# Pooled attention and capacity-limited experts on one core: another order for attention's first tiles

## Chip, core and metric

The kernel runs on one core of a Trainium2 chip. The metric is the device time of one execution in microseconds (us): 589.03 us is the median of three runs of the kernel before, which lie between 588.83 and 589.18 us. Times "at" a number are us from the start of the profiled span.

## The reference

Eight batch entries of q, k and v, each with 8 heads, 576 positions and 64 dims, go through attention against keys and values that are averaged over 8 positions (576 become 72):

```python
k_p = k.reshape(B, H, Sp, pool, D).mean(axis=3)
v_p = v.reshape(B, H, Sp, pool, D).mean(axis=3)
scores = scale * np.matmul(q, k_p.transpose(0, 1, 3, 2))
attn = np.exp(scores - scores.max(-1)) ; attn /= attn.sum(-1)
attn_out = np.matmul(attn, v_p)
```

The result, 4608 tokens of 512 numbers, goes to a mixture of 8 experts. Logits `x @ w_gate` are sorted over all tokens and experts, each expert takes at most 576 tokens, each token goes to one expert, and each expert computes `relu(x @ w1[e]) @ w2[e]` for its tokens.

## The kernel before

**Attention** works on 36 tiles of 128 tokens, in order. A batch entry is 4.5 tiles, so every ninth tile boundary falls on an entry's end, and tiles 4, 13, 22 and 31 hold the end of one entry and the beginning of the next. For tile n the steps are, with the names that the profile uses:

- `st_s` (scores): 4 matmuls of q (`rawq`) against the pooled keys in block-diagonal form (`kblk`), into the PSUM tile `pss`, of which there is one. The next tile's scores can only start when this tile's have been read.
- `softmax`: VectorE (DVE in the profile) takes the maximum (`mx`) and subtracts it (`e`), ScalarE (ACT) takes the exponential.
- `st_e`: five transposes of `e` through TensorE (PE), three into `pse`, two into `rt`, and a copy of each group to SBUF (`eT`) by ScalarE.
- `st_av`: five matmuls of `eT` against the masked pooled values (`vblk`, with the gate's 8 columns and a column for the sum of the weights) into one of two tiles `psa`.
- `norm`: VectorE divides by the sum (`rinv`, `gt`, every fourth tile `lg`, and `xt`); ScalarE's queue stores the tile.

In the loop over n, PE's queue holds `st_s(n)`, `st_e(n-1)`, `st_av(n-2)`, and VectorE's `mx(n)`, `e(n)`, `norm(n-3)`. Everything is written by hand in this order (a manual schedule), and each engine executes its own queue in order. A wait at the head of a queue holds up all that stands behind it.

**Pooling.** k, v and q of an entry are loaded by SyncE's queue (SP). The keys of an entry (`rawk`, 128 x 4 x 8 x 72) are summed in three steps, lines 173, 174 and 177; the last writes `kblk`. The values (`rawv`, 128 x 5 x 512, five chunks) are summed in three steps, lines 186 to 188 (`t`, `t`, `vsum`); three masked products, line 196, spread `vsum` over `vblk`. `prep_v` (three transposes of `vsum`, L209, and ScalarE's copy `vT`) and `prep_g` (three matmuls with the gate's weights, L218, and VectorE's product L219, "put" below) make the gate's columns of `vblk`. GpSimd (POOL) does k and v of entries 1 to 7. For entry 0, VectorE pools three quarters of k, TensorE the fourth (`add_k`); VectorE pools chunks 0 to 2 of v, and TensorE, with an identity matrix, chunks 3 and 4 (`add_v`, L156, with ScalarE's `put_v`).

**Constants** for the routing that follows are made in `consts` (before k of entry 0 is pooled) and `more` (after it), mostly on VectorE.

**After attention** come routing (a search for each expert's threshold) and the experts' matmuls, lines 1178 to 1266. Neither is touched.

Of the kernel before, what the change touches and what calls it, by code (L numbers as in the profile page):

```python
# [22 lines left out]
class Attention:  # L23
# [102 lines left out]
    def cut(self, b):  # L126

        return 256 + 64 * (b % 2)
# [7 lines left out]
    def q_of(self, b, j, n, m):  # L136

        c = self.cut(b)
        o = j * c + n if n < c else 4 * c + j * (self.S - c) + n - c
        return self.qT[b][:, o:o + m]  # L140
# [11 lines left out]
    def add_v(self, b, c):  # L152

        ps = self.ps0[:, 1, 128:256].rearrange("p (c d) -> p c d", c=2)
        for t in range(8):
            self.nc.tensor.matmul(ps, self.ident, self.rv[b][:, c, 64 * t:64 * t + 64], start=(t == 0), stop=(t == 7))  # L156

    def put_v(self, b, c):
        nc, B = self.nc, self.BLOCKS
        ps = self.ps0[:, 1, 128:256].rearrange("p (c d) -> p c d", c=2)  # L160
        self.sums[b] = self.wk.tile([128, 5, 64], F32, name="vsum")
        nc.scalar.activation(self.sums[b][:, c], ps, AF.Copy)
        for m in range(c.start, c.stop):
            for n in range(B[m], B[m + 1]):
                nc.scalar.activation(self.vblk[b % 4][:, n, :64], ps[:, m - c.start], AF.Copy, scale=self.mask[:, n:n + 1])

    def pool_k(self, b, eng, halves=(slice(0, 4),)):

        src = self.rk.pop(b)
        t1 = self.wk.tile([128, 4, 4, 72], F32, name="tk1", bufs=1)  # L170
        t2 = self.wk.tile([128, 4, 2, 72], F32, name="tk2", bufs=1)
# [7 lines left out]
    def pool_v(self, b, eng, c=slice(0, 5), blocks=None):  # L179
# [3 lines left out]
        t1 = self.wk.tile([128, 5, 256], F32, name="t1", bufs=1)  # L183
        t2 = self.wk.tile([128, 5, 128], F32, name="t2", bufs=1)
        s, v, B = self.sums[b], self.vblk[b % 4], self.BLOCKS
# [27 lines left out]
    def prep_g(self, b):  # L213
# [115 lines left out]
    def run(self, ctx, full, consts, more, after, end, warm):  # L329
# [7 lines left out]
        self.pS, self.e, self.eT, self.pA = {}, {}, {}, {}  # L337
        nt, B, S = self.nt, self.B, self.S
# [7 lines left out]
        mid = {}  # L346

        kh = (slice(0, 2), slice(2, 4))
        vh = (slice(0, 3), slice(3, 5))
        n = 4 * self.cut(0)  # L350
        self.load_k(0, kh)
        self.load_q(0, slice(0, n))
        self.load_v(0, vh[::-1])
# [1393 lines left out]
```

## Time and profile before

| | |
|---|---|
| median of three runs | 589.03 us |
| profiled execution | 588.63 us |
| its span, first to last instruction | 586.8 us |
| TensorE busy | 570.1 us (97% of the span) |
| VectorE, ScalarE, GpSimd busy | 392.1, 264.9, 176.5 us |
| mean granted TensorE clock | 0.987 |

The span leaves out 1.8 us of the execution. A busy share says how long an engine had an instruction in it, with overlaps; it doesn't say that the engine set the time in a given stage. For that the reader needs the order in time: which engine stood still, and what it stood still for. The rows further down are taken from the timeline (start, duration, engine, line, operation, output<-input, and in brackets the idle time before it and what ended it), from groups by line, from the chain of waits, and from the DMA issues.

### The profile page before, as it was taken

The numbers are of one execution on the slowest core, as the hardware profiler recorded it, in microseconds if no ns is written. First come the engines' busy times: TensorE is split into PE (matmuls) and PEld (weight loads), VectorE is DVE, ScalarE is ACT, GpSimd is POOL, SyncE is SP. The second block draws the span as 40 slices with busy tenths as digits, with TensorE's granted clock in tenths as the row PEclk, the third lists the DMA queues.
The fourth block names the chain that finished last, engine by engine and source line by source line (L and its number), as shares of the span: only waits on it lengthen the run. The fifth ranks groups of instructions, "written<-read, shape, count | busy, mean of one in ns | idle before, by whom it ended". The sixth has DMA issues, their size and how long they took to land.

```text
span 586.8 us, 10400 instructions
## 1 busy us (share of the span) xinstructions
PE 570.1 (97%) x3699; PEld 469.3 (80%) x3699; DVE 392.1 (67%) x1145; ACT 264.9 (45%) x528; POOL 176.5 (30%) x222
## 2 busy tenths in 40 slices
PE   8999999995999999999999999999999999999996
PEld 5999999893798889879976777678768868876874
DVE  7677878898897779687964886396658517421500
ACT  6444545444462445453462455246325724642401
POOL 1999999300300510420312302130121123011012
PEclk9999999997899999999999999999999999999999
DMA  8999982122550875568373926574484749165011
GB/s 352 421 422 422 396 349 80 77 83 72 169 196 3 267 192 174 165 180 286 110 167 89 360 67 161 181 269 123 94 298 132 165 152 327 57 162 196 12 41 45
DMA packets 74204, 110.25 MB, mean 188 GB/s; under 512 B 40640, under 2 KB 40640, under 8 KB 71456
## 3 DMA queue, kind: packets, MB, share of 16 engines
q1 hardware_dynamic: 62864, 81.02, 41.8%
q0 software_dynamic: 5952, 19.01, 9.6%
q10 hardware_dynamic: 5328, 9.48, 4.2%
q8 instruction: 30, 0.49, 0.3%
q14 instruction: 30, 0.25, 0.1%
HBM read 72.53 MB, written 27.92 MB: 171 GB/s over the span
## 4 chain that ended last, share of the span: by engine, by line
PE 79%; issue 6%; DVE 5%; POOL 4%; DMA 3%; ACT 0%; SPq 0%; POOLq 0%; another core or an unknown queue 0%; DVEq 0%; ACTq 0%
PE h L1261 25%; PE h L1215 16%; PE h L1178 14%; PE psa L273 6%; PE pss L228 5%; PE h L1266 4%; PE h L1204 3%; DMA rawk<-in_k_dram 2%; PE pse L257 1%; PE rt L666 1%; PE rt L257 1%; POOL tk L173 1%; DMA out_dram<-yt,rows 1%; DVE marks L659 1%; PE rt L218 1%
## 5 line engine op out<-in xcount | busy, mean ns | idle before, releaser
L1261 PE MATMUL h<-w2l,hh 128*128 128x512 f32 x256 | 101.0, 395 | 0.0
L1261 PE MATMUL h<-w2h,hh 128*128 128x512 f32 x256 | 100.7, 393 | 0.1
L1261 PE MATMUL h<-w2h,hl 128*128 128x512 f32 x256 | 100.8, 394 | 0.0
L1241 POOL DMA_INDIRECT out_dram<-yt,rows x29 | 28.9, 995 | 227.8 <-ACT yt L1275 227.3
L1090 POOL DMA_INDIRECT xg<-xd,rows x40 | 39.8, 996 | 85.8 <-ACT w1h L1098 28.1
L273 PE MATMUL psa<-vblk,eT 128*128 128x146 f32 (+3 forms) x390 | 60.0, 302 | 0.2
L1102 DVE TENSOR_TENSOR w1l<-raw,w1h 128x512 fp32r<-128x512 f32 x64 | 41.8, 685 | 24.4 <-ACT w1h L1098 23.9
L1261 PEld LDWEIGHTS h<-w2h,hh 128*128 128x128 f32 x256 | 48.2, 188 | 9.8 <-issue 0.5
L1261 PEld LDWEIGHTS h<-w2l,hh 128*128 128x128 f32 x256 | 48.2, 188 | 9.3
L1261 PEld LDWEIGHTS h<-w2h,hl 128*128 128x128 f32 x256 | 48.2, 188 | 9.2
L1275 ACT ACTIVATE yt<-h 128x512 f32<-128x512 f32 x32 | 19.0, 595 | 78.4 <-PE h L1261 54.7
L1220 ACT ACTIVATE hh<-h 128x512 fp32r<-128x512 f32 x40 | 23.9, 598 | 64.6 <-PE h L1215 64.6
L273 PEld LDWEIGHTS psa<-vblk,eT 128*128 128x128 f32 (+1 forms) x390 | 50.9, 180 | 1.8 <-POOL kblk L177 0.3
L1215 PE MATMUL h<-xh,w1h 128*128 128x512 f32 x160 | 45.2, 397 | 0.0
L1221 DVE SCALAR_TENSOR_TENSOR hl<-h,hh 128x512 fp32r<-128x512 f32 x40 | 27.4, 684 | 26.5 <-ACT hh L1220 26.4
L228 PE MATMUL pss<-kblk,rawq 128*128 128x144 f32 (+1 forms) x320 | 43.7, 294 | 1.4 <-DVE e L239 1.2
L1215 PE MATMUL h<-xl,w1h 128*128 128x512 f32 x160 | 43.8, 392 | 0.0
L1215 PE MATMUL h<-xh,w1l 128*128 128x512 f32 x160 | 43.6, 392 | 0.0
L1111 DVE TENSOR_TENSOR w2l<-raw,w2h 128x512 fp32r<-128x512 f32 x64 | 42.4, 681 | 0.0
L1098 ACT ACTIVATE w1h<-raw 128x512 fp32r<-128x512 f32 x64 | 37.0, 625 | 11.4 <-DMA raw<-in_moe_w_dram 11.2
L228 PEld LDWEIGHTS pss<-kblk,rawq 128*128 128x128 f32 (+1 forms) x320 | 37.0, 179 | 4.5 <-issue 2.5
L1108 ACT ACTIVATE w2h<-raw 128x512 fp32r<-128x512 f32 x64 | 37.9, 626 | 0.0
(240 smaller groups left out, 1107.0 us busy)
## 6 DMA issues: line engine op xcount, KB each, us to landing
raw<-in_moe_w_dram SPq DMA_DIRECT2D x64, 512.0 KB, 6.5
xd<-xt ACTq DMA_DIRECT2D x36, 256.0 KB, 3.9
rawv<-in_v_dram SPq DMA_DIRECT2D x7, 1280.0 KB, 13.7
rawk<-in_k_dram SPq DMA_DIRECT2D x7, 1152.0 KB, 12.9
rawq<-in_q_dram SPq DMA_DIRECT2D x7, 1152.0 KB, 10.2
xs<-planes SPq DMA_DIRECT2D x31, 256.0 KB, 2.9
rawk<-in_k_dram SPq DMA_DIRECT2D x2, 576.0 KB, 4.8
xs<-planes SPq DMA_DIRECT2D x7, 128.0 KB, 2.7
```

The source lines that it names most:

```text
L228: nc.tensor.matmul(ps[cols, j // 2, 144 * (j % 2):144 * (j % 2) + 144], self.q_of(b, j, n, cols.stop - cols.start), self.kblk[b % 4][:, j] ...
L273: self.nc.tensor.matmul(o[h], self.eT[i][:, c, h], self.vblk[b % 4][:, self.BLOCKS[c]:self.BLOCKS[c + 1]], start=(c == cs[0]), stop=(c == ...
L1090: nc.gpsimd.indirect_dma_start(out=self.xg[:n, t, :], out_offset=None, in_=self.xd, in_offset=bass.IndirectOffsetOnAxis(ap=rows[:n, t:t + ...
L1098: self.nc.scalar.activation(h, raw, AF.Copy)
L1102: self.nc.vector.tensor_tensor(l, raw, h.bitcast(F32), op=OP.subtract)
L1108: self.nc.scalar.activation(self.w2h[:, i], self.raw2[e][:, i], AF.Copy)
L1111: self.nc.vector.tensor_tensor(self.w2l[:, i], self.raw2[e][:, i], self.w2h[:, i].bitcast(F32), op=OP.subtract)
L1178: nc.tensor.matmul(ps[:, :m], a[:, n % 4, fs], b[:, n % 4, o], start=(n == 0), stop=(n == 11))
L1215: nc.tensor.matmul(ps, a[:, j, fs], b[:, j, :512], start=(n == 0), stop=(n == 11))
L1221: later(0.85, 0.69, lambda f=f, ps=ps: nc.vector.scalar_tensor_tensor(hl[:, f, :512], ps, 0.0, hh[:, f, :512].bitcast(F32), op0=OP.max, op ...
L1241: st = nc.gpsimd.indirect_dma_start(out=rows, out_offset=bass.IndirectOffsetOnAxis(ap=idx, axis=0), in_=y, in_offset=None)
L1261: nc.tensor.matmul(ps, a[:, f, o], b[:, f], start=(f == 0 and k == 0), stop=(f == 7 and k == 2))
```

## The change

q of entry 0 comes in three pieces instead of two (tokens 0 to 255, 256 to 383, the rest); the second now stands in front of v. For entry 1 q's first piece stands in front of v. Scores of tiles 0, 1 and 2 are issued in a row, tile 1's into a tile `psa`. `add_v` and `put_v` are gone: GpSimd pools chunks 3 and 4 and then 1 and 2 of entry 0's v, VectorE chunk 0. Of entry 1, VectorE pools the second half of k and chunk 4 of v, GpSimd the rest. `st_av` of tiles 0 and 1 follow after the scores of tile 3. `most` is the maximum alone, so that a put can stand between maximum and subtraction. Entry 2's `prep_v` and `prep_g` move one tile later. Constants of `consts` and `more` go to GpSimd, apart from three integer operations that VectorE now does before it pools k.

```diff
+    def cuts(b, S):
+        return (0, 256, 384, S) if not b else (0, 256 + 64 * (b % 2), S)
...
+    def most(self, i):
         ps = self.pS.pop(i)[:, :, :288].rearrange("p g (h y) -> p g h y", h=4)
         mx = self.wk.tile([128, 2, 4], F32, name="mx")
+        self.nc.vector.tensor_reduce(mx, ps, axis=AX.X, op=OP.max)
+        self.mx[i] = ps, mx
...
-        self.load_q(0, slice(0, n))
+        self.load_q(0, slice(0, 1024), slice(1024, 1536))
         self.load_v(0, vh[::-1])
-        self.load_q(0, slice(n, 4 * S))
+        self.load_q(0, slice(1536, 4 * S))
...
+        self.load_k(1)
+        self.load_q(1, slice(0, n))
+        self.load_v(1)
+        self.load_q(1, slice(n, 4 * S))
...
+            plan(n, self.pool_k, b, nc.gpsimd, (slice(0, 4 if b > 1 else 2),))
+            plan(n, self.pool_v, b, nc.gpsimd, slice(0, 5 if b > 1 else 4))
...
+        self.st_s(0)
+        self.st_s(1, "psa", 2)
+        self.pool_v(0, nc.gpsimd, vh[1])
+        self.pool_v(0, nc.gpsimd, slice(1, 3))
+        self.softmax(0)
+        self.st_s(2)
+        self.softmax(1)
+        self.pool_v(0, nc.vector, slice(0, 1))
+        self.blocks(0)
+        for n in range(2):
...
+            self.st_e(n, 0)
+            self.st_e(n, 1)
+        self.prep_v(0)
+        self.softmax(2)
+        self.st_s(3)
+        put = self.prep_g(0)
+        self.most(3)
+        put()
+        self.st_e(2, 0)
+        self.st_e(2, 1)
+        self.st_av(0, 0)
+        self.st_av(0, 1)
+        self.softmax(3)
+        self.pool_k(1, nc.vector, kh[1:])
+        self.st_av(1, 0)
+        self.st_av(1, 1)
+        self.norm(0)
+        self.pool_v(1, nc.vector, slice(4, 5))
+        self.blocks(1)
...
+        at_v = {first[b] + (b == 2): b for b in range(2, B)}
+        at_g = {first[b] + 1 + (b <= 2): b for b in range(1, B)}
+        for n in range(4, nt):
             self.st_s(n)
...
-        nc.vector.tensor_scalar(self.tri, jp, 0.0, None, op0=OP.is_gt)
+        nc.gpsimd.tensor_scalar(self.tri, jp, 0.0, None, op0=OP.is_gt)
```

First place: VectorE's queue from the last constants (before) and from the last keys (after) up to the third tile. `td`, `dq`, `tq` and `qcol` are constants of the routing, `t_` and `vsum` belong to the pooling of v, `mx` and `e` to the softmax. Before:

```order
L521 TENSOR_SCALAR td<-jp 128x4
L523 TENSOR_SCALAR dq<-td 128x4
L525 TENSOR_SCALAR tq<-pq 128x1
L527 TENSOR_SCALAR qcol<-tq 128x1
L238 TENSOR_REDUCE mx<-pss 128x8
L239 TENSOR_TENSOR e<-pss,mx 128x576
L186 TENSOR_TENSOR t_308<-rawv 128x768
L187 TENSOR_TENSOR t_309<-t_308 128x384
L188 TENSOR_TENSOR vsum<-t_309 128x192
L238 TENSOR_REDUCE mx<-pss 128x8
L239 TENSOR_TENSOR e<-pss,mx 128x576
```

And in the changed kernel:

```order
L168 TENSOR_TENSOR kblk_137<-tk_241 64x72 x2
L229 TENSOR_REDUCE mx<-pss 128x8
L238 TENSOR_TENSOR e<-pss,mx 128x576
L229 TENSOR_REDUCE mx<-psa 128x8
L238 TENSOR_TENSOR e<-psa,mx 128x576
L177 TENSOR_TENSOR t_289<-rawv 128x256
L178 TENSOR_TENSOR t_290<-t_289 128x128
L179 TENSOR_TENSOR vsum<-t_290 128x64
L229 TENSOR_REDUCE mx<-pss 128x8
L238 TENSOR_TENSOR e<-pss,mx 128x576
L229 TENSOR_REDUCE mx<-pss 128x8
```

The constants no longer stand between the keys and the first maximum, the pooling of v is a third as wide, and it has moved behind the second softmax.

Second place: VectorE's queue around the first `norm` (RECIPROCAL, `gt`, `xt`) and the maximum of tile 4. Before:

```order
L285 RECIPROCAL rinv<-psa 128x8
L288 TENSOR_TENSOR gt_432<-psa,rinv 128x64
L298 TENSOR_TENSOR xt<-psa,rinv 128x512
L238 TENSOR_REDUCE mx<-pss 128x8
L239 TENSOR_TENSOR e<-pss,mx 128x576
```

And in the changed kernel (`tk_` and `kblk_138` are entry 1's keys):

```order
L164 TENSOR_TENSOR tk_327<-rawk 128x576
L165 TENSOR_TENSOR tk_328<-tk_327 128x288
L168 TENSOR_TENSOR kblk_138<-tk_328 64x2x72 x2
L284 RECIPROCAL rinv<-psa 128x8
L287 TENSOR_TENSOR gt_405<-psa,rinv 128x64
L297 TENSOR_TENSOR xt<-psa,rinv 128x512
L177 TENSOR_TENSOR t_334<-rawv 128x256
L178 TENSOR_TENSOR t_335<-t_334 128x128
L179 TENSOR_TENSOR vsum<-t_335 128x64
L229 TENSOR_REDUCE mx<-pss 128x8
L238 TENSOR_TENSOR e<-pss,mx 128x576
```

Four instructions on entry 1's keys and three on its values now stand in front of tile 4's maximum.

Third place: SyncE's queue, the loads of entries 0 and 1. Before:

```order
L134 DMA rawq<-in_q_dram 128x1024
L124 DMA rawv<-in_v_dram 128x1024
L124 DMA rawv<-in_v_dram 128x1536
L134 DMA rawq<-in_q_dram 128x1280
L119 DMA rawk<-in_k_dram 128x2304
L124 DMA rawv<-in_v_dram 128x2560
L134 DMA rawq<-in_q_dram 128x2304
```

And in the changed kernel:

```order
L135 DMA rawq<-in_q_dram 128x1024
L135 DMA rawq<-in_q_dram 128x512
L124 DMA rawv<-in_v_dram 128x1024
L124 DMA rawv<-in_v_dram 128x1536
L135 DMA rawq<-in_q_dram 128x768
L119 DMA rawk<-in_k_dram 128x2304
L135 DMA rawq<-in_q_dram 128x1280
L124 DMA rawv<-in_v_dram 128x2560
L135 DMA rawq<-in_q_dram 128x1024
```

A piece of 128 x 512 (0.26 MB) stands before entry 0's v, and one of 128 x 1280 (0.66 MB) before entry 1's.

## Rows read from the trace of the kernel before

**Rows 1.** The page: busy time by engine; TensorE's granted clock in 40 equal slices of the span, in tenths; and the chain that ended last, by engine.

```profile
PE 570.1 (97%) x3699; PEld 469.3 (80%) x3699; DVE 392.1 (67%) x1145; ACT 264.9 (45%) x528; POOL 176.5 (30%) x222
...
PEclk9999999997899999999999999999999999999999
...
PE 79%; issue 6%; DVE 5%; POOL 4%; DMA 3%; ACT 0%; SPq 0%; POOLq 0%; another core or an unknown queue 0%; DVEq 0%; ACTq 0%
```

**Rows 2.** The chain of waits in order of time, its first long pieces: start, duration, what.

```profile
3.83 11.98 DMA rawk<-in_k_dram
15.88 2.63 POOL tk L173
...
21.80 2.91 POOL t L186
```

**Rows 3.** The timeline of the first 30 us: the first scores, VectorE from the last constants on, and the second scores.

```profile
7.95 1.29 PE L228 MATMUL pss<-kblk,rawq 128*128 128x144 f32 x8
...
8.26 0.23 DVE L492 TENSOR_SCALAR tri<-jp 128x128 bf16<-128x128 int32 x1
...
10.48 0.15 DVE L527 TENSOR_SCALAR qcol<-tq 128x1 f32<-128x1 int32 x1
...
10.56 0.75 DVE L238 TENSOR_REDUCE mx<-pss 128x8 f32<-128x576 f32 x1
11.34 0.76 DVE L239 TENSOR_TENSOR e<-pss,mx 128x576 f32<-128x576 f32 x1
12.01 0.95 DVE L186 TENSOR_TENSOR t<-rawv 128x768 f32<-128x768 f32 x1
...
12.24 1.22 PE L228 MATMUL pss<-kblk,rawq 128*128 128x144 f32 x8 [1.21 <-DVE e L239]
```

**Rows 4.** The timeline of TensorE's matmuls from 14 to 36 us (L228 scores, L257 transposes, L273 values, L209 and L218 the gate's columns), and the scores of tile 13.

```profile
21.92 1.20 PE L228 MATMUL pss<-kblk,rawq 128*64 128x144 f32 x16
23.05 0.60 PE L257 MATMUL pse<-ident,e 128*127 128x128 f32 x3
23.48 1.04 PE L273 MATMUL psa<-vblk,eT 128*128 128x146 f32 x6
24.36 0.38 PE L257 MATMUL rt<-ident,e 128*127 128x128 f32 x2
24.57 0.67 PE L273 MATMUL psa<-vblk,eT 128*128 128x146 f32 x4
25.08 1.14 PE L228 MATMUL pss<-kblk,rawq 128*128 128x144 f32 x8
...
28.27 0.52 PE L209 MATMUL rt<-ident,vsum 128*128 128x128 f32 x3
28.62 1.15 PE L228 MATMUL pss<-kblk,rawq 128*128 128x144 f32 x8
29.61 0.49 PE L257 MATMUL pse<-ident,e 128*127 128x128 f32 x3
29.94 0.74 PE L218 MATMUL rt<-wblk,vT 128*128 128x40 f32 x6
30.61 1.56 PE L273 MATMUL psa<-vblk,eT 128*64 128x146 f32 x12
...
33.17 1.25 PE L228 MATMUL pss<-kblk,rawq 128*128 128x144 f32 x8
...
52.68 1.24 PE L228 MATMUL pss<-kblk,rawq 128*64 128x144 f32 x16
```

**Rows 5.** GpSimd's pooling: the first line of k with the shortest, median and longest of its seven instructions in ns, two lines of v (busy us, mean ns), and the three masked products of entry 1 in the timeline.

```profile
L173 POOL TENSOR_TENSOR tk<-rawk x7: 2622/2628/2644, 15.9 to 94.4; 128x1152 f32<-128x1152 f32 x7
...
L186 POOL TENSOR_TENSOR t<-rawv 128x1280 f32<-128x1280 f32 x7 | 20.3, 2907 | 0.6
...
L187 POOL TENSOR_TENSOR t<-t 128x640 f32<-128x640 f32 x7 | 10.8, 1541 | 0.5
...
27.35 1.66 POOL L196 TENSOR_TENSOR vblk<-vsum,mask 128x128 f32<-128x128 f32 x3
```

**Rows 6.** SyncE's issues in order of time (start, duration): the two pieces of entry 0's v, and entry 3's v, which takes over the completion semaphore of entry 1's q and so is issued when that q has landed. Then two loads with us from issue to landing: the first piece of entry 0's v (issued at 2.17) and entry 2's k (issued at 6.08).

```profile
2.17 1.13 SPq L124 DMA_DIRECT2D rawv<-in_v_dram  x2
...
21.83 0.33 SPq L124 DMA_DIRECT2D rawv<-in_v_dram  x1
...
rawv<-in_v_dram SPq DMA_DIRECT2D x1, 512.0 KB, 6.5
...
rawk<-in_k_dram SPq DMA_DIRECT2D x1, 1152.0 KB, 18.8
```

**Rows 7.** The table by stretches: busy us by engine (instructions), granted clock, DMA's busy share and GB/s.

```profile
60.00:110.00 50.00, 49.94 (x408) 47.62 (x408) 41.03 (x90) 23.42 (x49) 46.60 (x39) 1.00 0.62 243
```

**Rows 8.** VectorE: the subtraction and two steps of the keys by form (busy us, mean ns), and the first and the last instruction of a `norm` in the timeline.

```profile
L239 DVE TENSOR_TENSOR e<-pss,mx 128x576 f32<-128x576 f32 x30 | 22.7, 758 | 2.9
...
L173 DVE TENSOR_TENSOR tk<-rawk 128x576 f32<-128x576 f32 x1 | 0.8, 758 | 0.0
...
L174 DVE TENSOR_TENSOR tk<-tk 128x288 f32<-128x288 f32 x1 | 0.5, 457 | 0.0
...
21.57 0.20 DVE L285 RECIPROCAL rinv<-psa 128x8 f32<-128x8 f32 x1
...
21.94 0.68 DVE L298 TENSOR_TENSOR xt<-psa,rinv 128x512 f32<-128x512 f32 x1
```

More of the change, by code (lines that the diff above doesn't have):

```diff
@@ L136, in q_of @@
     def q_of(self, b, j, n, m):
-        c = self.cut(b)
-        o = j * c + n if n < c else 4 * c + j * (self.S - c) + n - c
+        cuts = self.cuts(b, self.S)
+        for c0, c1 in zip(cuts, cuts[1:]):
+            if n < c1:
+                break
+        o = 4 * c0 + j * (c1 - c0) + n - c0
         return self.qT[b][:, o:o + m]
@@ L150, in add_k @@
             nc.scalar.activation(self.kblk[b % 4][h, j, y], ps[h], AF.Copy)
[L152 to L165, printed above, removed]
-    def pool_k(self, b, eng, halves=(slice(0, 4),)):
-        src = self.rk.pop(b)
-        t1 = self.wk.tile([128, 4, 4, 72], F32, name="tk1", bufs=1)
-        t2 = self.wk.tile([128, 4, 2, 72], F32, name="tk2", bufs=1)
+    def pool_k(self, b, eng, halves=(slice(0, 4),)):
+        src = self.rk[b]
+        if b not in self.tk:
+            self.tk[b] = (self.wk.tile([128, 4, 4, 72], F32, name="tk1", bufs=1),
+                          self.wk.tile([128, 4, 2, 72], F32, name="tk2", bufs=1))
+        t1, t2 = self.tk[b]
         for c in halves:
@@ L380, in run @@
             plan(first[b - 3] + 1, self.load_q, b)
-        for n in range(nt):
-            if n == 2:
-                self.prep_g(0)
-            self.st_s(n)
-            if n == 0:
-                self.add_v(0, vh[1])
-            for f in mid.get(n, ()):
-                f()
-            both = n >= 2 and len(self.parts(n - 2)) > 1 and n != first[1] + 2
-            if n >= 1:
-                self.st_e(n - 1, 0)
-            if n == first[1] + 2:
-                self.prep_g(1)
-            if n >= 2 and not both:
+        self.st_s(0)
@@ new lines, in run @@
+        self.most(3)
[11 more added lines that the diff above has]
+        self.blocks(1)
+        for n in (2, 3):
+            for f, a in at.get(n, ()):
+                f(*a)
+        at_v = {first[b] + (b == 2): b for b in range(2, B)}
@@ L396, in run @@
+        at_g = {first[b] + 1 + (b <= 2): b for b in range(1, B)}
+        for n in range(4, nt):
+            self.st_s(n)
+            both = len(self.parts(n - 2)) > 1
+            if n in at_v:
+                self.prep_v(at_v[n])
+            if n in at_g:
+                put = self.prep_g(at_g[n])
+                if n - 2 in first:
+                    self.most(n)
+                put()
+            self.st_e(n - 1, 0)
+            if not both:
                 self.st_av(n - 2, 0)
-            if n >= 1:
-                self.st_e(n - 1, 1)
+            self.st_e(n - 1, 1)
@@ L399, in run @@
             if both:
                 self.st_av(n - 2, 0)
[L401 to L404 removed]
+            self.st_av(n - 2, 1)
+            if n == first[1] + 1:
+                self.prep_v(1)
             self.softmax(n)
[L406 to L412 removed]
+            self.norm(n - 3)
@@ L413, in run @@
+            for f in after.get(n - 3, ()):
+                f()
             for f, a in at.get(n, ()):
```

121 lines of the change are left out of this document (55 added, 66 removed).

## The prediction

> **What bounds the kernel now.** I read the page first: TensorE is busy for 97% of the span and leads the chain for 79% of it [rows 1]. That doesn't tell whether attention's first 30 us, where everything that changes lies, are bound by it. So next the chain in order of time: from 3.8 to 29 us it doesn't run through TensorE but through the load of entry 1's k, which lands at 15.8, and then through GpSimd, which pools that k and, from 21.80, entry 1's v [rows 2]. Last the timelines. At the start VectorE is late: the first scores end at 7.95+1.29 = 9.24, but the maximum over them starts at 10.56, behind constants that run from 8.26 to 10.63, and the second scores wait until 12.24 for the subtraction [rows 3]. From 21.92 on TensorE runs without a gap worth the name, one tile in 3.1 us (21.92 to 25.08), up to 28.3; there it waits for entry 1's v, and tile 6's scores to tile 7's take 28.62 to 33.17, 4.55 us [rows 4]. After that the tiles go at an even pace again: six tiles in 52.68-33.17 = 19.5 us. The granted clock is in the top tenth in every slice up to 130 us [rows 1].
>
> Whatever time tile 7 gains is kept to the end if nothing before the experts runs on a clock of its own. DMA could; but from 60 to 110 us it is busy 0.62 while TensorE has 49.94 of 50 us [rows 7]. I take the gain as kept.
>
> **The change, step by step.** I follow the starts of the scores, since the one tile `pss` ties TensorE and VectorE together there.
>
> *Constants.* VectorE's stretch 8.26 to 10.56 goes [rows 3]. Three integer operations come in front of the keys, some 0.15 us each by the last constant's row, less three memsets: the keys end perhaps 0.2 later. The fourth quarter of k goes through TensorE and ScalarE and feeds the last score matmuls anyway, so I cost this at nothing; if it isn't covered it costs 0.2. The first maximum starts at 9.3 instead of 10.56. On GpSimd twelve short operations now stand before its first v, which lands at 9.3 (below). Seven are memsets and five tensor-scalar operations, of which the trace has none on GpSimd: if they end before 9.3 they cost nothing, else rival 4's price.
>
> *VectorE to the third softmax.* From maximum to subtraction 0.78, from subtraction to what follows 0.67 [rows 3]: 1.45 a tile. Tiles 0 and 1: 9.3+2.9 = 12.2. One chunk of v: 768 wide takes 0.95 [rows 3], the keys' 576 take 0.758 and 288 take 0.457 [rows 8], so about 0.17+0.00102 per element: 256, 128 and 64 wide take 0.43+0.30+0.23, 1.0 in all. Third softmax from 13.25; its subtraction ends at 14.8. The scores of tile 2 fit below it, from 10.95, when tile 0 has been subtracted.
>
> *GpSimd's v of entry 0.* The first piece of v landed at 2.17+6.5 = 8.7 [rows 6]. 0.26 MB of q now go ahead. The rate: entry 1's k lands at 15.8 [rows 2] and entry 1's q, after v and q with 2.49 MB, at 21.83 [rows 6]: 0.42 MB a us. So 0.6 us later, 9.3; the second piece, 0.79 MB, 1.9 later. GpSimd's 1280 wide take 2.91 and 640 take 1.54 [rows 5]: 0.18+0.00213 per element. Two chunks: 512, 256 and 128 wide, 1.27+0.73+0.46, with gaps 2.7. It ends at 12.0 and, for chunks 1 and 2, at 14.65. TensorE's `prep_v` stands in front of the scores of tile 3 and waits for it: 14.7, scores of tile 3 at 15.05 (the subtraction would have let them go at 14.85). The products to `vblk` take 1.66 [rows 5] and end at 16.3, in time.
>
> *To tile 4.* TensorE's pieces, from start to start [rows 4]: scores 0.98, first transposes 0.33 to 0.43, values 0.88, second transposes 0.21, values 0.5 to 0.6, gate matmuls 0.67. After 15.05: scores 0.98, gate 0.67, transposes 0.55, then the values need the put, which VectorE ends at about 17.3 (maximum from 16.25, 0.78, and the put, which I take as long as the 64-wide sum). From 17.35 two tiles of values at 1.5: scores of tile 4 at 20.35, against 21.92. Gain 1.55.
>
> *Tile 4 and 5.* VectorE meanwhile: subtraction of tile 3 to 18.0; half of k 0.76+0.46+2x0.31 = 1.8, to 19.75; `norm` 1.05 (21.57 to 22.62 [rows 8]), to 20.8; then it waits, if needed, for entry 1's v. That lands, behind 0.66 MB of q and its own 1.31 MB, at 15.8+1.97/0.42 = 20.5. Chunk 4 takes 1.0: maximum of tile 4 at 21.85, scores 5 at 23.4, and TensorE's own pace gives 20.35+3.1 = 23.45. Before 25.08: gain 1.6, with 0.3 us to spare on the load. GpSimd's half of k runs 16.3 to 19.7, in time for 20.35.
>
> *Tile 6 and 7.* GpSimd has four fifths of v: 2.36+1.27+0.73 and gaps, 4.6, from 20.5 to 25.1, products to 26.8. `prep_v` comes at 26.5 and no longer waits; scores 6 at 23.45+3.05+0.35 = 26.85. Then 0.98+0.67+0.55+1.5 = 3.7, a little waiting apart: scores 7 at 30.65, against 33.17. Gain 2.5. This is the old wait for entry 1's v, gone.
>
> *After.* Entry 2's k lands at 6.08+18.8 = 24.9 [rows 6], v some 3 us later; GpSimd starts on them at 26.8, ends at about 39.8, and needs to be done for the values of tile 9, at some 45. Its `prep` steps are only moved, same count; the pace to tile 13 is the old one, apart from one put that stands 0.1 to 0.2 late at tile 11. I take 2.4.
>
> Sum against the profiled execution: 588.63-2.4 = 586.2 (its span 586.8 becomes 584.4, and 1.8 lie around it). The median of three lies 0.4 above that execution, so 586.6.
>
> **The unknown: two engines in one memory.** In the trace no VectorE instruction with both inputs in SBUF runs beside a GpSimd instruction that reads SBUF; the nearest is the subtraction, one input in PSUM, at 758 ns [rows 8] with GpSimd's sums at 2622 to 2644 ns throughout [rows 5], so neither slows the other. The changed kernel sets such pairs side by side three times: chunk 0 of v, half of k, chunk 4 of v on VectorE, each while GpSimd sums. Bounds: below, no slowing (the nearest row), the sum above; above, each waits for the other's whole instruction (rivals 1 and 2). I take the row's.
>
> The Trainium skill says the opposite, in "SBUF — State Buffer", section "Who interferes with whom": a VectorE instruction with two SBUF inputs and a GpSimd instruction that reads SBUF share a port pair, and the later one is blocked until the first ends. No run here shows that case, and the row agrees with the same section's other half, that one SBUF input doesn't contend. By that rule the time would be rival 1's or 2's.
>
> **Rivals.**
>
> 1. *They take turns, an instruction each.* VectorE's chunk 0, due at 12.25, waits for the end of GpSimd's 512-wide sum, 12.0+1.27: 1.0 late, and scores 3 with it. Half of k, due at 19.0, meets GpSimd's half and waits 0.5; GpSimd's last steps of k then stand behind VectorE's 1.8, and scores 4 wait for them: another 1.0 in all. By 2.0 the gain shrinks to 0.4, and GpSimd's later pooling of entries 2 and 3 may cost up to 1 more. 588.2 to 589.6, say 589.0, no change. For it: the shared pieces are long on both sides. Against it: only that nothing in the trace shows it.
>
> 2. *VectorE loses each turn* (slower). GpSimd's instructions follow each other at gaps below 0.1 us. If it takes the next one before VectorE gets in, chunk 0 waits for 14.65 (2.4 late), half of k and what follows for the end of entry 1's v, at about 25.5, some 5.5 us after they were due. Scores 4 at 27.4, 5.5 behind before; what the old wait for v gives back is below 1. 588.63+5 and the 0.4: 594. It turns from faster to slower once VectorE's waits exceed 2.4 in all.
>
> 3. *Entry 1's v lands late.* A DMA wait now stands in VectorE's queue ahead of tile 4's maximum, and q's first piece ahead of that load. Each us past 20.8 costs one: landing at 22 gives 587.8, break-even is at 23.2. Against it: the rate of 0.42 MB a us held from 15.8 to 21.83.
>
> 4. *The first v is late on GpSimd* (constants slow, or a sum of 512 longer than the line through 640 and 1280). One for one on scores 3: 1 us gives 587.6, from 2.4 on nothing is left.
>
> **Chances.** Forecast 0.62, with its own range of 585.6 to 587.8 (0.5 us of pace and landing better, 1.2 worse); rival 1 0.18, rival 2 0.06, rival 3 0.09, rival 4 0.05. A change of 0.2%, 1.2 us, is about what can be told from none. Faster by more: 0.61 of the forecast, 0.06 of the others, 0.67. Slower by more: all of rival 2, 0.04 of rival 1, 0.04 of 3 and 4: 0.14. Within: 0.19. The range for 8 in 10 takes in rivals 1, 3 and 4 but not 2: 585.5 to 589.7.
>
> **What would show it.** First maximum at 9.3; `prep_v` of entry 0 released by GpSimd at 14.7; scores of tiles 3, 4, 5, 7 and 13 at about 15.05, 20.35, 23.45, 30.65 and 50.2; VectorE's 256- and 576-wide sums at 0.43 and 0.76 and GpSimd's 512- and 1024-wide at 1.27 and 2.36 even where they overlap. Longer ones there, or VectorE idle before its sums with GpSimd as releaser, speak for rivals 1 or 2; VectorE idle before chunk 4 with the load as releaser for 3. If the scores of tile 13 come earlier by 2.4 and the time doesn't, something behind attention has a clock of its own, and my step on the end is wrong.

## The result and the profile after

The changed kernel takes 592.8 us, median of six runs (591.79 to 594.53), beside 589.18 of the kernel before in the same comparison. The ratio is 1.0064 with an interval of 1.0049 to 1.008, so it is slower, by 3 to 5 us. The forecast was 586.6, faster, with a range up to 589.7: wrong in sign, and outside the range. The execution profiled below took 592.32 us, its span is 590.5.

The page, the lines that answer to [rows 1]: busy time by engine, the granted clock in 40 slices, the chain by engine.

```profile
PE 570.0 (97%) x3683; PEld 467.7 (79%) x3683; DVE 396.7 (67%) x1135; ACT 263.7 (45%) x523; POOL 182.6 (31%) x240
...
PEclk9999999997799999999999999999999999999999
...
PE 83%; DVE 8%; issue 7%; DMA 1%; POOL 1%; ACT 0%; POOLq 0%; another core or an unknown queue 0%; DVEq 0%; ACTq 0%
```

The shares hardly move. But in the chain GpSimd and DMA go from 4 and 3% to 1 and 1%, and VectorE from 5 to 8%: the old path through entry 1's k and v is gone, and VectorE is on the new one. Where, the timeline of TensorE shows, the lines that answer to [rows 4] (L221 scores, L256 transposes, L272 values).

```profile
16.36 1.25 PE L221 MATMUL pss<-kblk,rawq 128*128 128x144 f32 x8 [0.71 <-DVE e L238]
...
21.63 0.95 PE L221 MATMUL pss<-kblk,rawq 128*64 128x144 f32 x10
24.46 0.70 PE L221 MATMUL pss<-kblk,rawq 128*64 128x144 f32 x6 [1.88 <-DVE kblk L168]
...
28.21 1.22 PE L221 MATMUL pss<-kblk,rawq 128*128 128x144 f32 x8 [0.74 <-DVE rinv L284]
...
35.94 1.25 PE L221 MATMUL pss<-kblk,rawq 128*128 128x144 f32 x8
```

Tile 3's scores start at 16.36 (forecast 15.05), tile 4's at 21.63 (20.35). Then these stop in the middle: ten matmuls run, and the last six wait 1.88 us for VectorE's part of entry 1's keys. Tile 5 comes at 28.21 against 25.08 before, tile 7 at 35.94 against 33.17: 2.8 us lost where 2.5 were to be won. What VectorE and GpSimd do there, in their timelines (L164 to L168 are the keys' three steps, L177 to L179 those of v):

```profile
13.14 0.51 DVE L177 TENSOR_TENSOR t<-rawv 128x256 f32<-128x256 f32 x1
13.69 0.70 DVE L178 TENSOR_TENSOR t<-t 128x128 f32<-128x128 f32 x1
14.42 0.43 DVE L179 TENSOR_TENSOR vsum<-t 128x64 f32<-128x64 f32 x1
...
19.15 0.87 DVE L164 TENSOR_TENSOR tk<-rawk 128x576 f32<-128x576 f32 x1
20.05 0.63 DVE L165 TENSOR_TENSOR tk<-tk 128x288 f32<-128x288 f32 x1
20.72 3.68 DVE L168 TENSOR_TENSOR kblk<-tk 64x144 f32<-64x144 f32 x2
...
9.54 1.27 POOL L177 TENSOR_TENSOR t<-rawv 128x512 f32<-128x512 f32 x1 [2.40 <-DMA rawv<-in_v_dram]
...
13.45 0.79 POOL L178 TENSOR_TENSOR t<-t 128x256 f32<-128x256 f32 x1
...
20.45 2.45 POOL L177 TENSOR_TENSOR t<-rawv 128x1024 f32<-128x1024 f32 x1
22.98 1.26 POOL L178 TENSOR_TENSOR t<-t 128x512 f32<-128x512 f32 x1
```

And the tile `kblk` from 19 to 25 us: shortest, median and longest in ns. The third line is the same pair of sums for entry 0 in the kernel before, where GpSimd does nothing between 2.7 and 14.0 us.

```profile
L168 POOL TENSOR_TENSOR kblk<-tk x2: 488/698/907, 18.9 to 19.5; 64x144 f32<-64x144 f32 x2
L168 DVE TENSOR_TENSOR kblk<-tk x2: 1332/1834/2337, 20.7 to 23.1; 64x144 f32<-64x144 f32 x2
...
6.27 0.62 DVE L177 TENSOR_TENSOR kblk<-tk 64x144 f32<-64x144 f32 x2
```

Two sums of 64x144, some 0.30 us each where nothing runs beside them, last 2.34 and 1.33. The first, begun at 20.72, is done at 23.06; GpSimd's 1024-wide sum of v ends at 22.90. The second, begun at about 23.1, is done at 24.4; GpSimd's 512-wide one ends at 24.24. Neither waits on a semaphore: the time stands inside the instruction. Read alone, such a row says "a slow sum"; only GpSimd's rows beside it say that it stood still until the other engine's instruction ended. It goes the other way too: of GpSimd's two sums for `kblk` the first takes 0.49 us, and the second, begun at 19.46 beside VectorE's sum of 19.15 to 20.02, takes 0.91 and ends at 20.37.

### The profile page after: what moved, and what is told of

Read it like the earlier page. It is cut to its first block, busy times and chain, and to the rows that moved or that the text cites. A ratio compares the mean times of both kernels' runs of the same rounds, so it can differ in the third digit from the quotient of the medians.

```text
span 590.5 us, 10377 instructions
## 1 busy us (share of the span) xinstructions
PE 570.0 (97%) x3683; PEld 467.7 (79%) x3683; DVE 396.7 (67%) x1135; ACT 263.7 (45%) x523; POOL 182.6 (31%) x240
## 4 chain that ended last, share of the span: by engine, by line
PE 83%; DVE 8%; issue 7%; DMA 1%; POOL 1%; ACT 0%; POOLq 0%; another core or an unknown queue 0%; DVEq 0%; ACTq 0%
PE h L1286 25%; PE h L1240 16%; PE h L1203 13%; PE psa L272 6%; PE pss L221 6%; PE h L1291 4%; PE h L1229 3%; PE pse L256 2%; DVE e L238 1%; PE rt L691 1%; PE rt L256 1%; PE rt L562 1%; DVE mx L229 1%; PE rt L210 1%; DMA out_dram<-yt,rows 1%
## 5 line engine op out<-in xcount | busy, mean ns | idle before, releaser
L272 PE MATMUL psa<-vblk,eT 128*128 128x146 f32 (+3 forms) x390 | 58.9, 302 | 0.1
L272 PEld LDWEIGHTS psa<-vblk,eT 128*128 128x128 f32 (+1 forms) x390 | 50.6, 179 | 1.6 <-issue 0.3
L221 PE MATMUL pss<-kblk,rawq 128*128 128x144 f32 (+1 forms) x312 | 43.0, 295 | 4.2 <-DVE kblk L168 1.9
L221 PEld LDWEIGHTS pss<-kblk,rawq 128*128 128x128 f32 (+1 forms) x312 | 36.1, 179 | 8.1 <-issue 2.3
```

The costliest lines, as they stand in the source:

```text
L221: nc.tensor.matmul(ps[cols, j // 2, 144 * (j % 2):144 * (j % 2) + 144], self.q_of(b, j, n, cols.stop - cols.start), self.kblk[b % 4][:, j] ...
L272: self.nc.tensor.matmul(o[h], self.eT[i][:, c, h], self.vblk[b % 4][:, self.BLOCKS[c]:self.BLOCKS[c + 1]], start=(c == cs[0]), stop=(c == ...
```

## The experiments

**One input instead of two.** VectorE's three shared sums become one reduction each; the host lays these pieces out for it, outside the measured time, and ScalarE copies the keys' reduction into `kblk`.

```diff
-        self.pool_v(0, nc.vector, slice(0, 1))
+        self.red_v(0, slice(0, 1))
...
-        self.pool_k(1, nc.vector, kh[1:])
+        self.red_k(1)
...
-        self.pool_v(1, nc.vector, slice(4, 5))
+        self.red_v(1, slice(4, 5))
...
+        nc.vector.tensor_reduce(t, self.rk[b][:, 2:4].rearrange("p c t y -> p c (t y)")
+                                .rearrange("p c (y t) -> p c y t", t=8), axis=AX.X, op=OP.add)
```

> The changed kernel, but the three sums that VectorE takes beside GpSimd (entry 0's first chunk of v, half of entry 1's k, entry 1's last chunk of v) are one reduction each, with a single input in SBUF; the host lays these pieces out so that the eight rows to be added are neighbours. GpSimd's share, the order on TensorE and the loads are the changed kernel's. Theory (a VectorE instruction with two SBUF inputs can't run beside a GpSimd sum and waits for its end): no VectorE instruction is stretched any more, the two 64x144 sums of the keys that took 3.68 us are gone, tile 4's scores run in one piece, scores of tile 7 at 31 to 32 (35.9 in the changed kernel), time 586.5 to 588. Rival (VectorE's queue is simply too long or in the wrong order there, whatever the instruction): scores of tile 7 stay at 35 to 36, time 592 to 593.

588.1 us (ratio 0.9985, 0.9975 to 0.9994), 0.1 over the expected range; tile 7 as expected. VectorE's timeline, with TensorE's scores of tiles 4 and 7:

```profile
13.13 0.68 DVE L196 TENSOR_REDUCE vsum<-rawv 128x64 f32<-128x512 f32 x1
18.17 1.34 DVE L185 TENSOR_REDUCE tk<-rawk 128x144 f32<-128x1152 f32 x1
...
20.65 1.20 PE L239 MATMUL pss<-kblk,rawq 128*64 128x144 f32 x16
...
31.49 1.25 PE L239 MATMUL pss<-kblk,rawq 128*128 128x144 f32 x8
```

The same pooling at the same places on the same engines, and tile 4's sixteen score matmuls run in one piece; tile 7 is 4.45 us earlier than in the changed kernel. The order of VectorE's queue isn't the cause. Its length is a small part at most: the three reductions take 2.7 us (0.68, 1.34, 0.68) where the sums were costed at 3.8 without a neighbour. The rest is two-input sums that stand still beside GpSimd.

**The lock by itself**, that is, a VectorE instruction held until GpSimd's ends. In the kernel before, unused VectorE instructions stand beside GpSimd's pooling of entries 4 to 7.

```diff
+        if k == 0:
+            nc.vector.tensor_tensor(pr, pa, pb, op=OP.add)
+        elif k == 1:
+            nc.vector.tensor_scalar(pr, pa, 2.0, None, op0=OP.mult)
+        else:
+            nc.vector.tensor_reduce(pr[:, :32], pa.rearrange("p (d t) -> p d t", t=8), axis=AX.X, op=OP.add)
...
+            if 14 <= n < 32:
+                self.probe(n % 3)
```

> The kernel before with one more VectorE instruction in each of tiles 14 to 31, whose result nobody reads, 128x256 fp32 in SBUF, while GpSimd pools entries 4 to 7: in turn a tensor-tensor sum (two SBUF inputs), a tensor-scalar product (one) and a reduction of 256 to 32 (one). Theory (lock on two SBUF inputs): sums that start beside a GpSimd sum last until its end, up to 2.9 us, and 0.43 where GpSimd is idle; products and reductions last the same with and without GpSimd. Rival (any VectorE work on SBUF slows down beside GpSimd): products and reductions are stretched as well. Rival (no lock; tile 4's two instructions waited for something else): all sums at 0.43 to 0.5.

The tile by operation (shortest, median, longest in ns):

```profile
L209 DVE TENSOR_REDUCE pr<-pr x6: 408/409/412, 60.0 to 111.4; 128x32 f32<-128x256 f32 x6
L205 DVE TENSOR_TENSOR pr<-pr,pr x6: 415/506/1519, 63.4 to 114.7; 128x256 f32<-128x256 f32 x6
L207 DVE TENSOR_SCALAR pr<-pr x6: 283/588/873, 66.5 to 119.4; 128x256 f32<-128x256 f32 x6
```

Three of these in the timeline, with what GpSimd runs beside them:

```profile
81.27 2.65 POOL L173 TENSOR_TENSOR tk<-rawk 128x1152 f32<-128x1152 f32 x1
82.68 1.52 DVE L205 TENSOR_TENSOR pr<-pr,pr 128x256 f32<-128x256 f32 x1
...
85.55 1.64 POOL L177 TENSOR_TENSOR kblk<-tk 64x288 f32<-64x288 f32 x2
86.62 0.72 DVE L207 TENSOR_SCALAR pr<-pr 128x256 f32<-128x256 f32 x1
...
90.26 1.55 POOL L187 TENSOR_TENSOR t<-t 128x640 f32<-128x640 f32 x1
90.57 0.41 DVE L209 TENSOR_REDUCE pr<-pr 128x32 f32<-128x256 f32 x1
```

The sum begun at 82.68 ends at 84.20, 0.28 after GpSimd's instruction (83.92). The reductions take 0.41, five beside GpSimd and one alone. The products were a surprise: one input, and stretched all the same, 0.28 us alone (one of the six) and 0.52 to 0.87 in the other five, each to the end of GpSimd's instruction and 0.15. So "one input" is not the rule for what is free; the reduction is, and the product isn't. (The execution took 591.71.)

**Entry 1 wholly on GpSimd.**

```diff
-            plan(n, self.pool_k, b, nc.gpsimd, (slice(0, 4 if b > 1 else 2),))
-            plan(n, self.pool_v, b, nc.gpsimd, slice(0, 5 if b > 1 else 4))
+            plan(n, self.pool_k, b, nc.gpsimd)
+            plan(n, self.pool_v, b, nc.gpsimd)
...
-        self.pool_k(1, nc.vector, kh[1:])
-        self.pool_v(1, nc.vector, slice(4, 5))
```

> The changed kernel, but entry 1's k and v are pooled wholly on GpSimd, as in the kernel before; entry 0's v stays split. So two of the three places where both engines sum side by side are gone. Theory (lock): GpSimd ends entry 1's k at about 22.6, so scores of tile 4 come at 22.6 instead of 21.6 but in one piece, scores of tile 5 at 25.5 to 26, scores of tile 7 at 32 to 33, time 588 to 589.5, about the kernel before: the split costs 3 to 4 us more than it saves. Rival (the three tiles in a row or the order of loads is what costs): time stays at 591.5 to 593.

591.9 us: a miss, and a time in the rival's range. But the rival's cause isn't it, for one_input keeps the three tiles in a row and the loads and is faster than the kernel before; and up to tile 7 this run went nearly as expected (tile 5 at 25.54, tile 7 at 33.18, as before). The 3.2 us of its span (590.0 against 586.8) are lost further on. The marks, routing's first matmuls after attention (`rt<-oh,marks`), start 0.70 later (133.96 against 133.26). From there to the first expert matmul (`h<-xh,w1h`) it is 21.21 us, against 20.50. The other 1.8 come behind it (1.2 of them within the first forty expert matmuls), where the clock in this profile is still low. First this run, then the kernel before (TensorE's first expert matmuls, and a stretch of 3 us from there, as in the table of [rows 7]):

```profile
155.16 1.22 PE L1199 MATMUL h<-xh,w1h 128*128 128x256 f32 x4
155.00:158.00 3.00, 2.95 (x15) 2.84 (x14) 2.79 (x15) 0.11 (x1) 0.00 (x0) 0.50 0.28 100
...
153.76 0.74 PE L1178 MATMUL h<-xh,w1h 128*128 128x256 f32 x4 [0.25 <-ACT xh L1153]
154.00:157.00 3.00, 3.00 (x27) 3.00 (x27) 2.79 (x15) 0.47 (x1) 0.00 (x0) 1.00 0.32 111
```

The granted clock is 0.50 (1.2 GHz) and not 1.00 (2.4 GHz), and 15 matmuls fit in where 27 did. Being level at tile 7 was not enough.

**The constants alone.** The kernel before, with routing's constants made by GpSimd as in the change (those of `more` and three memsets of `consts`; the others of `consts` stay on VectorE in both).

```diff
-        nc.vector.tensor_scalar(self.tri, jp, 0.0, None, op0=OP.is_gt)
+        nc.gpsimd.tensor_scalar(self.tri, jp, 0.0, None, op0=OP.is_gt)
```

> The kernel before with one part of the change, routing's constants on GpSimd. Entry 1's k and then its v on GpSimd lead in the kernel before up to tile 7, so an earlier first maximum shouldn't reach the end: 588.6 to 589.6, the same. If GpSimd's constants are in themselves harmful (they delay GpSimd's first sums or the warm-up), scores of tile 7 come later than 33.2 and the time is over 590. The warm-up matmuls of the changed kernel ended at 7.27 instead of 6.29; if GpSimd's constants cause that, it shows here too, else it ends near 6.3.

589.47, ratio 1.0003 (0.9992 to 1.0013): the same. The first maximum starts at 9.22 and tile 7 at 32.21, a us earlier than before, since entry 1's k landed 0.8 earlier in this execution; by the marks 0.67 of that is left, at the end nothing.

**Either half of the cure.** In only_k the chunk of entry 0's v stays as two-input sums; its edit against one_input:

```diff
-        self.red_v(0, slice(0, 1))
+        self.pool_v(0, nc.vector, slice(0, 1))
```

In only_v0 the half of entry 1's k and the last chunk of its v stay:

```diff
-        self.red_k(1)
+        self.pool_k(1, nc.vector, kh[1:])
...
-        self.red_v(1, slice(4, 5))
+        self.pool_v(1, nc.vector, slice(4, 5))
```

> The changed kernel with reductions in the place of VectorE's half of entry 1's k and of entry 1's last chunk of v; entry 0's first chunk of v stays as two-input sums beside GpSimd. Theory: the chunk costs some 0.9 us at tile 3 (16.4 against 15.5 in one_input) and that is all, so tile 7 at 32.2 to 32.5 and time 588.5 to 589.5; the keys' two sums then account for the other 3.5 us at tile 7. Rival (the chunk's wait is the larger part): tile 7 at 34 or later, time over 590.5.

> The other half of only_k: the changed kernel with a reduction for entry 0's first chunk of v alone; half of entry 1's k and the last chunk of its v are two-input sums again. Theory: tile 3 at 15.2 to 15.5 as in one_input; one of the keys' sums then waits for GpSimd's sum of v again (to 22.4 or later), tile 4's scores stop in the middle, tile 7 at 34.5 to 35.7, time 591 to 592.5. Rival (without the chunk's delay VectorE's half of k fits in before GpSimd starts on v): tile 7 at 32 or earlier, time under 589.

only_v0: 591.91 (591.16 to 592.79), tile 3 at 14.98, tile 7 at 34.50. As the theory had it:

```profile
17.68 1.30 DVE L164 TENSOR_TENSOR tk<-rawk 128x576 f32<-128x576 f32 x1
...
19.68 2.90 DVE L168 TENSOR_TENSOR kblk<-tk 64x144 f32<-64x144 f32 x2
...
22.63 0.70 PE L239 MATMUL pss<-kblk,rawq 128*64 128x144 f32 x6 [1.52 <-DVE kblk L168]
```

only_k: 592.71, a miss, and an instructive one. Four of ten runs lie at 588.6 to 589.3, as expected, with a mean clock of 0.986 to 0.988; six at 592.6 to 593.9, at 0.975 to 0.981. The profile is one of the six. Its table by stretches (busy us and instructions of TensorE, weight loads, VectorE, ScalarE, GpSimd, then granted clock, DMA share, GB/s):

```profile
13.00:16.00 3.00, 1.34 (x8) 0.94 (x8) 2.90 (x5) 2.10 (x6) 2.68 (x6) 0.99 1.01 419
16.00:22.00 6.00, 5.56 (x23) 5.53 (x24) 3.21 (x5) 2.06 (x5) 5.71 (x6) 0.50 1.02 424
```

And its timeline, the scores of tile 3:

```profile
16.44 2.29 PE L239 MATMUL pss<-kblk,rawq 128*128 128x144 f32 x8 [0.85 <-DVE e L256]
```

TensorE, kept waiting for the chunk, is busy 1.34 of 3 us; then the clock is at 0.50, 1.2 instead of 2.4 GHz, for 6 us in which it works almost without a gap: eight score matmuls take 2.29 us, 1.25 in the changed kernel. Tile 4 comes at 24.64, against 20.65 in one_input. That the other five of the six runs went the same way is inferred from their mean clocks. And the gap alone doesn't decide it: gp_entry1's profile has the same 1.34 us in the first stretch, and the clock stays up in the second.

```profile
13.00:16.00 3.00, 1.34 (x8) 0.94 (x8) 2.90 (x5) 2.13 (x6) 2.68 (x6) 1.00 1.02 419
16.00:22.00 6.00, 5.68 (x41) 5.27 (x41) 2.87 (x7) 2.02 (x4) 5.78 (x5) 1.00 1.01 421
```

**The gaps filled.** only_k with 16 unused matmuls in these gaps.

```diff
+        def fill(n):
+            for _ in range(n):
+                nc.tensor.matmul(self.ps0[:, 1, 128:384], full, full[:, None].to_broadcast([128, 2, 128]),
+                                 start=True, stop=True)
```

> only_k with 16 matmuls of 256 columns, whose result nobody reads, in the gaps of TensorE between 11 and 16.4 us. only_k had two groups of times, 588.6 to 589.3 (clock 0.986 to 0.988) and 592.6 to 593.9 (0.975 to 0.981); its profile, of the slow group, shows the clock at 0.50 from 16 to 22.4, after a stretch from 13 to 16.4 in which TensorE was busy for less than half. Theory (the gaps that the wait for the chunk leaves let the clock fall): all runs at 587.5 to 589.3, none over 591. Rival (the fall has nothing to do with the gaps): about half of the runs over 591 again. The 16 matmuls also move the fetch of TensorE's code back, worth 0.5 or so.

588.78, ten runs at 588.68 to 590.25, six of them within 0.1; none over 591. The same two stretches:

```profile
13.00:16.00 3.00, 2.68 (x23) 2.25 (x22) 2.90 (x6) 2.13 (x5) 2.68 (x6) 1.00 1.01 419
16.00:22.00 6.00, 5.42 (x43) 5.24 (x42) 4.00 (x8) 3.13 (x8) 5.71 (x6) 1.00 1.01 421
```

Work that nobody needs keeps the clock up and takes 4 us off six runs of ten. The further 0.5 us didn't come: 588.8 is no better than only_k's four lower runs.

**Both kernels once more**, unchanged.

> The kernel before, profiled once more. Between the first matmul over the marks after attention and the first expert matmul lay 20.50 us in its profile, but 20.9 to 21.2 in those of const_only, gp_entry1, one_input and the changed kernel. Theory A (this stretch varies from execution to execution by up to a us): anything from 20.5 to 21.2 here. Theory B (the change itself lengthens this stretch): 20.5 again. Tile 7's scores should start at 33.2 again in both.

> The changed kernel, profiled once more. The lock has to show again: one VectorE sum of the keys, 64x144, that lasts until a GpSimd sum of v ends (2 to 3 us instead of 0.30), and scores of tile 4 that stop in the middle. If the warm-up's matmuls end at 5.9 instead of 7.3, as in gp_entry1 and const_only, the start differs from execution to execution and isn't the change's. From the marks to the first expert matmul: 20.5 by theory A if this execution is a lucky one, 21.2 by theory B.

before_again: 588.91, tile 7 at 33.17, 20.75 us from the marks to the first expert matmul. after_again: 592.54, the same lock to 0.01 us (20.73, 3.68), 21.02 us for that stretch. So it varies by some 0.2 us from one execution of a kernel to the next (theory A), and is longer in the changed kernel in both of its profiles (theory B). after_again also shows one reason why the changed kernel's times spread over 2.7 us: VectorE's wait leaves TensorE idle from 22.6 to 24.46, and here the clock falls behind it, in the profile shown above it doesn't.

```profile
22.00:24.00 2.00, 0.59 (x8) 0.32 (x4) 1.99 (x2) 0.00 (x0) 1.92 (x2) 1.00 1.01 401
24.00:28.00 4.00, 3.54 (x15) 3.09 (x16) 3.76 (x10) 0.49 (x1) 3.35 (x6) 0.57 1.01 421
```

It costs 0.54 there: tile 5 at 28.75 instead of 28.21. The spans differ by 0.3 only, so most of the spread has no profile that shows it.

**A shorter warm-up.** `warm(13)` becomes `warm(11)` in one_input.

> one_input with 11 warm-up matmuls instead of 13. If the late end of the warm-up (7.3 in one_input's profile, 5.9 in others) is what holds the first tile there, the first sums of k start at 6.1 to 6.4 instead of 7.07, tile 0's scores at 8.0 to 8.4, tile 3 no earlier than GpSimd's v allows (15.1), and the time gains 0.3 to 0.8: 587.3 to 587.9. If the first tiles wait for GpSimd's v anyway, or if the shorter warm-up leaves the clock low for longer, no gain: 588 to 588.6.

587.9 (ratio 0.9983, 0.9973 to 0.9994), tile 0's scores at 8.12, tile 3 at 15.19, tile 7 at 31.17. Thirteen warm-up matmuls ended at 5.9 in gp_entry1 and const_only, at 7.3 in the changed kernel and one_input: this varies, and is worth 0.3 at tile 7. In the time it can't be told from one_input's: the two intervals overlap.

**Behind attention.** Four more variants of one_input_w11 look for what is lost from the marks on. fetch_back and filled have about as many TensorE instructions as the kernel before; dve_pad has as many VectorE instructions ahead of the marks as that; both_pad is fetch_back with dve_pad's edit. fetch_back:

```diff
-        warm(11)
+        warm(17, m=2)
+        warm(10, m=1)
```

filled, whose fillers are those of only_k_fill:

```diff
-        warm(11)
+        warm(10)
+        warm(4, m=1)
...
+        fill(4)
         self.st_s(2)
...
+            if n:
+                fill(6)
...
+        fill(3)
         self.prep_v(0)
```

dve_pad:

```diff
+        for _ in range(17):
+            nc.vector.memset(pad, 0.0)
         self.most(3)
```

> one_input_w11, whose 11 warm-up matmuls of 512 columns become 27 of 256 and 128 columns, 5632 columns as before: 32 more instructions on TensorE (16 matmuls and their weight loads), as many as the change took out with the first sums of v that TensorE made. Theory: a block of TensorE's code is fetched by a DMA; in the six profiles without these 32 instructions that DMA comes 16 us after the first matmul over the marks, among the loads of the first expert's tokens, and the tokens land 4.4 to 4.7 us after their issue; in the four with them it comes at 11 us and the tokens land after 3.4 to 3.8. So here the fetch at 11, the tokens 3.4 to 3.8 us after their issue, marks to first expert matmul 20.5 to 20.9 instead of 21.26, and 587.0 to 587.4. Rival (the stretch is longer for another reason, such as loads): 21.0 to 21.3, time 587.7 to 588.

> one_input_w11 with 13 such matmuls in the gaps before the transposes and prep_v, and the warm-up as 10 matmuls of 512 and 4 of 128 columns: together again 32 more instructions on TensorE. If both theories hold: clock 1.00 to 130 us in every run, fetch at 11, and a narrower group of times at 587.0 to 587.4, none over 588.5 (one_input_w11 had 587.4 to 589.6). If the fillers get in the way: scores of tile 3 later than 15.3.

> one_input_w11 with 17 more VectorE instructions (writes of zero to an unused 128x1) where VectorE waits for tile 3's scores, so that as many VectorE instructions as in the kernel before stand ahead of the marks. From the first matmul over the marks to the issue of the first gather of tokens lay 14.48 to 14.50 us in the six profiles with 238 or more of these instructions, and 14.75 to 14.79 in the eight with 233 or 235; these eight have a small fetch of code some 4 us after the marks, or nearly so. Theory (where VectorE's code is fetched costs this 0.29): 14.5 here, and time 0.3 below one_input_w11, 587.5 to 587.7. Rival (it is the constants on GpSimd or something else that goes with them): 14.8, and 587.9.

> dve_pad and fetch_back together: instructions ahead of the marks on VectorE as in the kernel before, and TensorE's fetch 11 us after the marks. From the marks to the first expert matmul: 20.5 to 20.8 as in the kernel before, and 587.0 to 587.3, if the two places of the code fetches make up what is lost between attention and the experts; 21.0 or more and 587.5 or more if fetch_back's 4.7 us from the gather's issue to its landing were no accident and the loads are late for another reason.

The 32 instructions do move a packet of code (the DMA view's larger queue of kind "instruction", 30 packets and 0.49 MB in the changed kernel) from 16 to 11 us after the marks, in all three variants that have them. The rest is undecided. TensorE takes up the first tokens 4.74 us after GpSimd issues their gather (`xg<-xd,rows`) in fetch_back, against expectation, 4.23 after it in filled, and only in both_pad 3.62 after, with 20.88 us from marks to experts. The times: fetch_back 588.08 (ratio 0.9983, 0.9974 to 0.9993) and filled 587.86 (0.9978, 0.9969 to 0.9987), both over what was expected; dve_pad 587.9 (0.9979, 0.997 to 0.9988); both_pad 587.62 (0.9979, 0.9969 to 0.9989). dve_pad's theory falls: 14.75 from marks to gather, not 14.5. With one_input_w11 at 587.9, the places of the code fetches are worth 0.3 us at best.

The profiles of fetch_back, filled and dve_pad have something else in common: each is of the highest run of its kernel (589.29, 589.29, 589.16), and in each the first four expert matmuls take 1.20 to 1.22 us, as in gp_entry1, and start 21.84 to 22.21 us after the marks. So these runs, 1.2 to 1.4 us above their medians, are ones in which the low clock behind attention lasts into the experts. What decides that, no run shows.

both_pad is faster than both kernels, as one_input and its other variants are, whose intervals all lie below 1: 0.2% under the kernel before, and so some 5 us under the changed one.

## Why the prediction was wrong

- *The unknown, two engines in one memory: the step that failed.* I took no slowing, from a row in which one of VectorE's inputs lies in PSUM, and kept the other value for rivals at 0.24. The probe shows a two-input sum standing still to the end of GpSimd's instruction; without such sums one_input gets back 4.45 of the 5.3 us between my tile 7 (30.65) and the measured one, of which its shorter instructions can explain 1.1 at most. By the Trainium skill, "SBUF — State Buffer", section "Who interferes with whom", a VectorE instruction with two SBUF inputs contends with a GpSimd instruction that reads SBUF, and the later one blocks fully: the traces agree (2.34 us for a sum of 0.30). The same section names `tensor_scalar` as able to contend and says that `tensor_reduce` never does here: the probe agrees with both (up to 873 ns for 283; 408 to 412 throughout). A nearest row that differs in exactly the disputed property was no evidence against a rule about that property.
- *Which rival it was.* Rival 1's rule, a turn each, at nearly rival 2's price: 592.8 against 594. Rival 1 put 2.0 us on the waits since it let half of k meet only GpSimd's half of k. In truth VectorE's short sums come to stand against GpSimd's longest as well, those of v, one for one: half of k with the turn lasts 5.25 us (19.15 to 24.40), not 1.8. With 0.65 more on the chunk (1.7 against 1.0) the waits are 4.1; rival 2's break-even was 2.4, and 1.7 of the 2.8 lost at tile 7 follow from that; one_input too comes to tile 7 0.8 later than forecast, and 0.3 no run separates. By only_v0 (34.50) and one_input_w11 (31.17) entry 1's part costs 3.3 at tile 7; the chunk has the rest, 0.9 by only_v0 (35.94-34.50, less the 0.5 that the changed kernel's first scores came later: 8.88 against 8.37), or 1.1 as what is left of 4.45.
- *Constants: right in size.* The first maximum comes at 9.22 in const_only (forecast 9.3), at 10.22 in the changed kernel, where the warm-up ended 1.4 us later (7.27 against 5.85). GpSimd's constants end at 7.1, and its first sum then waits 2.40 us for the load: rival 4 is out.
- *GpSimd's durations: right.* 1.27, 0.73, 0.46, and for 1024 wide 2.45 beside the two-input sums and 2.36 beside one_input's reductions (forecast 2.36), as the line through two widths had it.
- *Entry 1's v: right.* GpSimd starts on it at 20.45 without a wait for a load: rival 3 is out.
- *The path to tile 7 without the lock: right to 0.5 in one_input_w11, to 0.8 in one_input, whose warm-up ended later.* one_input_w11 has tile 3 at 15.19, tile 4 at 20.34, tile 5 at 23.51, tile 7 at 31.17; forecast 15.05, 20.35, 23.45, 30.65. The mechanism paid for, three tiles in a row and shared pooling, works up to tile 7 once VectorE's share is a reduction.
- *"The gain is kept to the end": a second step that failed, by about a us.* Within attention it holds: the changed kernel's 2.8 at tile 7 is 2.7 at the marks. Behind them it doesn't: 2.7 becomes 3.7 at the end of the span, and one_input's gain of 1.7 becomes 0.6. In both, 0.5 to 0.7 is lost between the marks and the first expert matmul (21.23 and 21.21 us, 20.50 and 20.75 in the two profiles of the kernel before). Part of it lies where the first tokens are gathered:

```profile
133.26 0.57 PE L666 MATMUL rt<-oh,marks 128*128 128x16 bf16 x17
147.74 0.97 POOL L1090 DMA_INDIRECT xg<-xd,rows  x1 [1.29 <-DVE rows L853]
151.55 1.78 PE L1151 MATMUL tp<-ident,xg 128*128 128x128 f32 x8
```

```profile
135.97 0.57 PE L691 MATMUL rt<-oh,marks 128*128 128x16 bf16 x17
150.46 0.98 POOL L1115 DMA_INDIRECT xg<-xd,rows  x1 [1.29 <-DVE rows L878]
155.20 1.31 PE L1176 MATMUL tp<-ident,xg 128*128 128x128 f32 x8 [0.90 <-issue]
```

The first is before_again, the second the changed kernel: marks, issue of the gather, first use of the tokens. To the issue it is 14.48 and 14.49; from there to the use 3.81 and 4.74. The code packet at 16 us goes with the longer of the two in all eight profiles that have it (4.45 to 4.74); of the eight with the packet at 11 us six have 3.43 to 3.81, but two 4.23 and 4.74. The times don't bear it out, so the cause stays open.

What made the prediction wrong, then, is one term that stood in the sum at nothing: the waits of two-input sums, 3.5 us in half of k and 0.7 in the chunk. The us behind attention adds to it, without changing the sign.

## What to carry to other kernels

Before a pooling is split between VectorE and GpSimd, ask of each VectorE instruction whether it stands still beside a GpSimd sum: here a two-input sum in SBUF did, and a product with a constant, while a reduction didn't; and what it loses is what is left of GpSimd's instruction, whatever its own length. Where no trace shows the disputed case, a written rule about just that case weighs more than a nearest row that lacks it. And a wait that leaves TensorE idle costs more than its length where the clock falls behind it, which it did in some executions and not in others.

## What the runs showed that I had not expected

- A VectorE product with one SBUF input and a constant stands still beside GpSimd as well (up to 0.87 us for 0.28), while a reduction with one input doesn't (0.41 in all six, five of them beside GpSimd).
- Gaps made 4 us in only_k a matter of chance: TensorE busy 1.34 of 3 us, then 6 us at 1.2 GHz in the profile, and times 4 us higher in six runs of ten; with 16 unused matmuls in the gaps it was none of ten.
- 32 more TensorE instructions at the start bring a code packet's load, which comes over 130 us later, forward by 5 us. Whether that gains anything the runs don't settle.
- The low clock behind attention lasts into the experts in five of the sixteen profiles (gp_entry1, only_k, fetch_back, filled, dve_pad): their first four expert matmuls take 1.20 to 1.22 us, 0.73 to 0.74 in the other eleven.
